# S4D convolution by FFT and gated MLP, f32: exchanges by quarters placed one by one, a decay table of 27 values, and a new order of the first phase

## The chip, the cores and the metric

One core of a Trainium2 chip runs the kernel; everything is f32. The metric is the device time of one execution in microseconds, as the median of several runs. Beside it there is one profiled execution, from which every duration below comes.

## What is computed

`x` is 2048 x 512. A layernorm, a long convolution per channel whose kernel is a sum of 128 decaying oscillations, and then a gMLP block with a spatial product over the sequence:

```python
P = jnp.exp((A * dt[:, None])[:, :, None] * pos)       # A = -exp(log_A_real) + i A_imag
K = 2.0 * jnp.einsum("dn,dnl->dl", C, P).real          # the convolution kernel of each channel
y = jnp.fft.irfft(jnp.fft.rfft(u_t, L2) * jnp.fft.rfft(K, L2), L2)[:, :, :L]
h = x + y + u * D_skip                                  # u is layernorm(x)
z = gelu(layernorm(h) @ w_in); z1, z2 = z[..., :Fh], layernorm(z[..., Fh:])
return h + (z1 * (w_sp @ z2 + b_sp)) @ w_out
```

## The kernel before

The change lies in the first phase, `phase_a`, which does the convolution; the three phases behind it (products with `w_in`, the second half of it with its norm, and the spatial product with the output) are as they were, and their lines have numbers smaller by 7 in the changed file (the line of the loads of `xq` is L715 before and L708 after).

The channels go in four chunks `c`. Per chunk:

- `params` turns the raw parameters into rates, phases and weights; three words per oscillation go to DRAM and come back through `stack` into `sw`. `table` makes `mt`, 64 by 34 values per partition: GpSimd multiplies the decay rates by a list of 34 distances (`c_lt`, three instructions), ScalarE takes the Exp, GpSimd multiplies four of the columns by the weights.
- Eight `unit`s (numbered `su` = 0 to 31 over all chunks) make the convolution kernel: a matmul for the phases (`ps<-c_k,sw`), Sin on ScalarE, three products of `mt` columns on GpSimd (`wa<-mt`), products on VectorE (`f`, `wa`) and GpSimd (`wb`), and two groups of 16 small matmuls (`ps<-f` and `ps<-wa,wb`), whose sum goes to a `ks` tile.
- `norm_x` normalises the input; 64 of its rows go to ScalarE or to GpSimd, one by one. `piece_a` and `piece_b` are the two matmul steps of the forward transform of the input, `piece_c` (`ps<-wb,ks`) and `piece_d` (`ps<-big,a`) those of the convolution kernel. Behind each `piece_d` its result is multiplied into the input's spectrum in `trio`, by VectorE; in chunk 3 three of the eight pieces are copied by ScalarE and multiplied by GpSimd, two instructions each. `piece_e` (`ps<-c_inv,trio`) is the inverse transform.
- `exchange(c)` swaps the two halves of the partitions of the input's spectrum, from one third of `trio` into another: 2 MB by DMA from SBUF to SBUF. Up is partitions 64 to 127 into 0 to 63, down the reverse; each in four quarters by `d`. All multiplies of `piece_d(c)` need it. Its target is still read by `piece_e(c-1)`: quarter q by the pieces `e(c-1, 2q)` and `e(c-1, 2q+1)`.

The order is not that of the code. `phase_a` records its operations in a `Plan`; a `group` counts as one operation. `RANKS` gives each its place, `FORMS` the engine where a copy or a normalised row may go to two, `BANKS` the PSUM bank. Up to `cut`, the last operation that touches the tiles which the next phase's loads will overwrite, all five queues are issued in that order. Then `phase_b1` issues its loads on SyncE: xq0, g0, xq1, g1 (a megabyte each), four quarters of w1r (448 KB each), xq2. Only then the rest of the plan is issued, with SyncE's instructions no longer held to the plan's order, and among it pieces of the split of w1r.

In `exchange`, the down half (a group) gets a dependency on the last DMA of the up half; SyncE waits there until that has landed. This is the key `after` in `issue`.

All recorded operations show the one line L252 (L251 after) in the profile.

Of the kernel before, what the change touches and what calls it, by code (L numbers as in the profile page):

```python
# [12 lines left out]
AF = mybir.ActivationFunctionType  # L13
# [24 lines left out]
    "06030B0I2U0Z0s10111I1N1j2619344U5V21000D0201050407080A090F0G0K0L0N0U0a0c0i0k0E0n1B0t0u0M0v14161A1G1d0O0Q0P0Y0b0dA10p0w0q"  # L38
    "1217181F1P1c1k1z282H2Q1e2X2R2V2v350r1H1J1L1s1-0H0C0W0l0J0V1E1m0R1t3G2Y3g3f0S1Y0X1Z234S4Y0T1i1f2g2s0o0e0j0g0m0x0f0h0z130y"
    "0-1Q0+1D151n1S1O1X1M1W1K1C1q1R1o1l1b1U1a1V1x1y24292A2z2B2C2G2J2N2T2Z2c2e2k2m2q2u2+2y3Z3W3l323B3A37333L3a314a4C4k393I3K4T"  # L40
    "67494B4N3e4A4G5x3J383y3b4j3V43483H2l2-1h272a3M3O1w2D2L1r1v2K3S2w1u2d3P2S2O2o2E2h2i2M3R2p3Q2t3N2W3E3T3U3X3Y3k3j3m3n3o3q3w"
    "3x3-42454F4I4P4V4b4W4f4n4z524c6f4s5c5P4q736u4t4-4v4m4o5E6O536e5U6v5v6o606n6U575D5a5+5C4g59867q7z9S9Q1T1p2P303i3u3z3+1g22"
    "20252F2IE82j2x2r3C3D3c3d3p404D4E4M4d6V4e5t4R5T708D3F365e7A7b7e46474X5g6N6Y6g7O7P5F5G5H5M5X5zJv6A6j6T6x7M7N7S7Y7d7j7t7u9-"
    "BB8hAKBJBKBLBeCmE27B7l8UBDBgBzBUBfBt5k5l6K6L5Q5S5N5O5R5Y5u5w5Z5d62636r728F8G7L7R8O8P7p807n7o8R8S6S6Z8V9u2f1+2n4J4O4l3h3t"
    "3v4H4w4Z4x4y6-8a8b2b3s4K4h4i4p3r41444Q564r5K5L5f7v814u584+515455505A5I5B5s5W5y5-7i9W9d5J5b5m5h5i5j5n5o5q5p6B616E6J797w85"
    "7F784L7f7Q7+7-5r6D6G68696P6C6F6X6W6a6b6c6i7C8M8N646d6M65666H6Q6R6q6k6t6s6y758I9V9X7g6h6w87888K6p767H7E8W7I8d8f8x94956I6z"
    "6+6l6m717V7W7m7k7r7x828C8l92938T8E7c9b7h9v9w8n8s7T7U7y8B74777X7Z7J7K7a7s7D7G8y9A8t919D9E9f9m9Y9ZANAOAQAU9k9oA8A9AqB2B1B6"
    "9sA6ASATABAC9rA29n9zCaCwBIBYBrBsCoC+BvCBCYCjCWCeBuCKCpDI8L8e8z8i8j8k8q968u9L8v8-98909M9i9jBFBP8J8483898A8X8Z8H8g8Q8c8Y8o"
    "8m8r8wAEBcC09N9a9P9K9T9U9e9c9p9g9q9l9y9tAGAJB3BVBW9F9H998p8+979B9C9G9O9J9I9x9R9+A0BMBaBbBZBjAj9hBqC8CCAmAMAVAZAaAbAwAeA+"
    "AvArAxB9B4BGBHDrDvD+AHADA5A3A4A7AWAAAIAgAPAFAlAXAnAsCEDADBBoBmBkBdBhBiB+BwBpC3BnBlC1B-C4CGCfDZDaB5ApAoA-B0B8BNBQBECABCBA"  # L50
    "C2BOCHCJCVDWDXC9C7BXC6BTCFChAfAkAhALARAYAyAzB7AcAiAdBRBSCZAtAuBxD7D8D9ByC5EnDsDxEQEbEDERDVDfDEDLDUDYF0F1DkDqExEyEkElEHEt"
    "D-EBECEPEWEeEmEwE7EGFEFFGDGJFRG0FrG2GaGdG5GCGYGZFXFlGiGtCDCRCUCQCkClCzCqCxCrCvD5DCD6DGDHDJEvE+COCTCICLCMCNCgCSCPCXCcCbCd"
    "CnCsC-DMFpFuCyDRDcDODPDQDhDSDdDjDeDmDuDpDzEEFZFaFoCiCuCtD0D1D2DFD3DDD4DNDKDbDTDiDlEuFIFJEgETEFFdEYFeFiEAEIELDwE9ENEdEKEO"
    "EMEXEZEcEfEoEpHCHDHGE5E0DtDgDnDoDyEJE6ESE3E1EaE4EhEiEjGkGlEVEzF2EqErEsFCF4F5FPE-F3FQFDFYFcG8GeGfEUFGFKFHFLFSFvFWFVFjFbFT"
    "GFFwGLGXH7HAHBGwFmFBGKGbHiHjF6F8F7F9FAFMFNFUFOFfFsFgFqFxFtFzF+GPGmGrGcGjGsG-HIHLI9IAHgHxGuH1HHHYHkHvH8H9HrHtHQHhHsHuHyHz"
    "HmHnHPHlH+IBHoHqIHIXIjIsIkIxIGIZIEIFITIeIbIoICIDIlImFyFkFhF-G3G4GEG6G7GAG9GGGHGIGUGWJGJOJWFnGOGSG1GMGNGgGpGRH2GQGTGqGhH3"
    "H4HXJ2J3GBGVGyGnGvGxHEH0G+HOH5GzHNHJHbHcIYJ9JVHMHTHRGoH6HFHZHKHVHaHUHSHWHdHeHfHwH-I0HpIUIKI7IPIQIpIaISIrIVIRIuItIvIyJHJd"
    "JeI4I6IMI1I2IIIcI3IJI5ILINIWIdIfIzI-JIJXI+J4JFJ5J7J8JRJPJJJQJLJMJNJSJTJUJYJZJaIOIiInI8IgIhIwIqJAJ0J1J6JBJCJDJEJKJbJcJuJw"
    "JfJgJhJrJkJpJjJmJqJnJiJoJlJxJ+JzJyJ-JsJtKCKEK2K9K6KFK3KAK0K1K7K8K4K5KBKD"
)  # L60
FORMS = (
    "000000001010100011000011100100000101100000011000001000000111001100110000100000000000100111100001010101101111101000000001"
    "00000110110110010100000100100100001110010100000010000001000110001101001101100000000101101110001001100000111001101111"
)
BANKS = (
    "414220313014444030432220022044434342124120412142014001422000123112321121011031223434430243400423134324420430131103321432"
    "034214411300222000123324434132420203334344321432242224410132113203001432002102101211314313432104023143234243141003422442"
    "030104322301034014314303413333144024"
# [3 lines left out]
def constants():  # L72
# [40 lines left out]
    for i in range(8):  # L113
# [9 lines left out]
        24 - 8 * np.arange(4), 1 + np.arange(7), 7 - np.arange(8), 64 * (1 + np.arange(7)),  # L123
        32 + 8 * np.arange(4), 512 * np.arange(4),
    ]).astype(f8)
    c["c_lt"] = np.broadcast_to(-lt, (P, 34))
# [62 lines left out]
class Plan:  # L189
# [59 lines left out]
    def issue(self, o):  # L249
        r = None  # L250
        for e, method, args, kw in o["calls"]:  # L251
            r = getattr(getattr(self.nc, e), method)(*map(self.real, args), **{k: self.real(x) for k, x in kw.items()})  # L252
            if "after" in o:
                info = mybir.DependencyInfo(mybir.DependencyClass.Sync, mybir.DependencyReason.DATA)
                self.tc.add_manual_dep(r.ins, o["after"]["ins"].name, info, reason="half by half")
        o["ins"] = r.ins
        return r
# [1047 lines left out]
```

## Time and profile before

| | us |
|---|---|
| runs | 813.02, 815.15, 815.5; median 815.15 |
| the profiled execution | 815.59 |
| its span | 813.8 |
| first phase, by the end of e(3) | about 274 of the span |
| PE busy over the span | 766.2 |
| granted TensorE clock, mean | 0.993 |

PE is TensorE's matmuls, PEld its weight loads, which overlap; DVE is VectorE, ACT ScalarE, POOL GpSimd, SP SyncE, and SPq SyncE's queue, whose rows are DMA issues. A row of a timeline has start, length, instruction, and in brackets the idle time of the engine just before it with what ended it. `out<-in` names the tiles; one name stands for several buffers.

### The profile page before, as it was taken

How to read it: one execution, taken by the hardware profiler on the slowest of the kernel's cores; microseconds unless marked ns; L12 is line 12 of the kernel's file. 1: busy time of each engine (PE TensorE's matmuls, PEld its weight loads, DVE VectorE, ACT ScalarE, POOL GpSimd, SP SyncE). 2: the span in 40 equal slices, each digit the busy share in tenths (PEclk: the TensorE clock that was granted, in tenths of full speed). 3: DMA queues.
4: the chain of work that ended last, by engine and by line, in shares of the span. 5: the costliest groups of instructions: out<-in, count | busy, mean ns of one | idle time of the engine just before them, and what ended most of it. 6: DMA issues, size and time to landing. Idle time of an engine off the chain costs nothing.

```text
span 813.8 us, 20008 instructions
## 1 busy us (share of the span) xinstructions
PE 766.2 (94%) x8081; PEld 651.5 (80%) x8081; DVE 593.7 (73%) x1155; ACT 452.0 (56%) x809; POOL 308.2 (38%) x356
## 2 busy tenths in 40 slices
PE   2489999999988989999999999999999999999998
PEld 1257888889978977888999888888888888888887
DVE  8998987976663587652586799978848993887534
ACT  8999989788652394562232455564345442454111
POOL 8999999978455100000421002233221002231200
PEclk9999999999997999999999999999999999999999
DMA  7604514415049256542450247999898548799542
GB/s 260 210 13 155 120 44 109 111 51 108 11 93 398 81 129 173 141 170 91 122 152 11 79 128 177 204 213 238 169 225 212 154 132 191 167 254 259 126 116 78
DMA packets 65004, 119.48 MB, mean 147 GB/s; under 512 B 6800, under 2 KB 21264, under 8 KB 63632
## 3 DMA queue, kind: packets, MB, share of 16 engines
q1 hardware_dynamic: 53248, 96.71, 39.5%
q0 software_dynamic: 11664, 21.50, 16.2%
q8 instruction: 63, 1.03, 0.5%
q14 instruction: 29, 0.24, 0.1%
HBM read 90.40 MB, written 19.40 MB: 135 GB/s over the span
## 4 chain that ended last, share of the span: by engine, by line
PE 83%; ACT 7%; DVE 7%; issue 2%; POOL 1%; DMA 0%; DVEq 0%; ACTq 0%; POOLq 0%
PE m L1192 34%; PE ps L252 20%; PE pz L987 9%; PE pz L882 8%; PE po L1115 7%; PE pl L1115 2%; DVE trio L252 2%; ACT ps L252 2%; ACT big L252 2%; PE y L756 1%; ACT wb L252 1%; DVE f L252 1%; DVE ps L252 1%; POOL wa L252 1%; DVE big L252 1%
## 5 line engine op out<-in xcount | busy, mean ns | idle before, releaser
L1192 PE MATMUL m<-wts,zc_wa 128*128 128x512 f32 x700 | 221.3, 395 | 0.0
L1192 PEld LDWEIGHTS m<-wts,zc_wa 128*128 128x128 f32 x700 | 131.8, 188 | 31.1 <-DVE c L1207 0.4
L1063 POOL DMA_DIRECT2D raws<-in_w_sp_dram x64 | 58.1, 991 | 211.7 <-DMA raws<-in_w_sp_dram 205.3
L1192 PE MATMUL m<-wts,zc_wb 128*128 128x512 f32 x350 | 138.2, 395 | 0.0
L252 POOL TENSOR_TENSOR wa<-mt 128x512 f32<-128x512 f32 x96 | 106.6, 1127 | 12.3 <-DVE big L252 4.2
L690 ACT CAST wts<-raws 128x512 fp32r<-128x512 f32 x112 | 68.9, 619 | 50.6 <-PE m L1192 24.5
L691 DVE TENSOR_TENSOR wts<-raws,wts 128x512 fp32r<-128x512 f32 x112 | 76.9, 689 | 17.1 <-ACT wts L690 17.0
L1192 PEld LDWEIGHTS m<-wts,zc_wb 128*128 128x128 f32 x350 | 65.9, 188 | 15.4
L987 PE MATMUL pz<-w,ht 128*128 128x448 f32 x384 | 77.0, 362 | 0.0
L987 PEld LDWEIGHTS pz<-w,ht 128*128 128x128 f32 x384 | 72.1, 188 | 4.8
L882 PE MATMUL pz<-ht,w1h 128*128 128x512 f32 (+1 forms) x248 | 73.8, 377 | 1.0 <-ACT ht L839 0.7
L993 POOL TENSOR_SCALAR sm<-sm 128x1 f32<-128x1 f32 x16 | 5.4, 336 | 159.9 <-DVE sm L992 159.9
L690 ACT CAST zc_wa<-raws 128x384 fp32r<-128x384 f32 (+1 forms) x70 | 37.1, 533 | 46.7 <-DVE raws L1097 28.0
L252 PE MATMUL ps<-c_inv,trio 128*128 128x128 f32 x512 | 60.8, 278 | 1.9 <-DVE trio L252 1.4
L1115 PE MATMUL po<-w,gz 128*128 128x512 f32 x252 | 61.8, 393 | 0.0
L252 PEld LDWEIGHTS ps<-c_inv,trio 128*128 128x128 f32 x512 | 58.5, 192 | 3.3 <-POOL trio L252 1.6
L252 PE MATMUL ps<-big,a 128*128 128x128 f32 x448 | 57.9, 287 | 1.2 <-ACT big L252 0.7
L252 DVE TENSOR_TENSOR f<-ps,wa 128x512 f32<-128x512 f32 (+1 forms) x64 | 46.9, 752 | 14.5 <-ACT ps L252 12.7
L252 PEld LDWEIGHTS ps<-big,a 128*128 128x128 f32 x448 | 54.2, 199 | 3.6 <-DVE trio L252 0.9
L1115 PEld LDWEIGHTS po<-w,gz 128*128 128x128 f32 x252 | 47.3, 188 | 10.9 <-DVE zo L1155 0.4
L882 PEld LDWEIGHTS pz<-ht,w1h 128*128 128x128 f32 x248 | 45.2, 189 | 10.8 <-ACT ht L839 1.4
L1097 DVE TENSOR_TENSOR raws<-z 128x384 f32<-128x384 f32 (+1 forms) x80 | 45.9, 582 | 0.3
(158 smaller groups left out, 1437.4 us busy)
## 6 DMA issues: line engine op xcount, KB each, us to landing
raws<-in_w_sp_dram SPq DMA_DIRECT2D x112, 256.0 KB, 4.0
raws<-in_w_sp_dram POOLq DMA_DIRECT2D x80, 256.0 KB, 5.8
trio<-trio SPq DMA_DIRECT2D x32, 256.0 KB, 3.8
scr_z<-zo SPq DMA_DIRECT2D x28, 256.0 KB, 2.1
big<-in_u_a_dram SPq DMA_DIRECT2D x8, 512.0 KB, 5.9
xq<-in_u_b_dram SPq DMA_DIRECT2D x4, 1024.0 KB, 8.9
g<-in_c_g_dram SPq DMA_DIRECT2D x4, 1024.0 KB, 8.9
scr_h<-xq SPq DMA_DIRECT2D x16, 256.0 KB, 4.1
```

Of the source, the lines that this page charges most:

```text
L252: r = getattr(getattr(self.nc, e), method)(*map(self.real, args), **{k: self.real(x) for k, x in kw.items()})
L690: nc.scalar.copy(hi, src)
L691: (engine or nc.vector).tensor_tensor(lo, src, hi.bitcast(F32), op=ALU.subtract)
L756: nc.tensor.matmul(ys[n, g][o:o + 64, i, :], gs[n][w, l, r], qv[w, r, 16 * n + l], start=(r == 0), stop=(r == 1), tile_position=(64 * h, o))
L882: nc.tensor.matmul(pt[:, w], a[:, q, f], ht[n][k][:, q, w], start=((q, i) == terms[0]), stop=((q, i) == terms[-1]))
L987: nc.tensor.matmul(pt[:, :FQ], a[:, q], w2[:, b, q, f], start=(q == 0 and i == 0), stop=(q == 3 and i == 2))
L993: nc.gpsimd.tensor_scalar_add(sm[:, 14:15], sm[:, 13:14], 1e-5)
L1063: nc.gpsimd.dma_start(r, ws[1], accum_op=ALU.add)
L1097: nc.vector.tensor_tensor(zs[:, :w], x, y, op=op)
L1115: nc.tensor.matmul(pt, gz[fb][x][:, P * a:P * a + P], wo[:, y, fb, w], start=(first and fb == fbs[0] and i == 0), stop=(last and fb == fbs ...
L1192: nc.tensor.matmul(pt, x[:, f], y, start=(k == 0 and i == 0), stop=(k == KT - 1 and i == 2))
```

## The change

1. `exchange` records eight operations where it recorded two groups of four. Up and down come in turn, quarter by quarter; the dependency of the down half on the up half is gone, and each of the eight has its own rank.
2. `c_lt` has 27 columns instead of 34: the two runs 1 to 7 and 7 to 0 shared values, and the second is now read backwards. The three GpSimd products of a table and the Exp shrink to 27/34.
3. In `params` the two sines stay in PSUM, and the three products with them go from GpSimd to VectorE.
4. `RANKS`, `FORMS` and `BANKS` are new throughout. In `FORMS`, 27 of the 64 normalised rows go to GpSimd instead of 23. ScalarE loads 19 activation tables in the first phase instead of 16.

```diff
 RANKS = (
-    "06030B0I2U0Z0s10111I1N1j2619344U5V21000D0201050407080A090F0G0K0L0N0U0a0c0i0k0E0n1B0t0u0M0v14161A1G1d0O0Q0P0Y0b0dA10p0w0q"
+    "0G020k0p2i0K0a0-111S1a1-220b4b3x3Q0J05010B000A1004070806090C0D0E0F0R0S0T0c0e0I0g0n0i0j0H0m14151F1G1I0L0N0M0O0P0Q2O0X0Z0Y"
...
     lt = np.concatenate([
-        24 - 8 * np.arange(4), 1 + np.arange(7), 7 - np.arange(8), 64 * (1 + np.arange(7)),
-        32 + 8 * np.arange(4), 512 * np.arange(4),
+        24 - 8 * np.arange(4), 1 + np.arange(7), 64 * np.arange(8), 32 + 8 * np.arange(4), 512 * np.arange(4),
     ]).astype(f8)
...
-            if "after" in o:
-                info = mybir.DependencyInfo(mybir.DependencyClass.Sync, mybir.DependencyReason.DATA)
-                self.tc.add_manual_dep(r.ins, o["after"]["ins"].name, info, reason="half by half")
...
-        si = ai
+        si, cp = bank("si", [P, N]), bank("co", [P, N])
...
-        nc.scalar.activation(co, a, AF.Sin, bias=half_pi)
+        nc.scalar.activation(cp, a, AF.Sin, bias=half_pi)
...
-        nc.gpsimd.tensor_tensor(co, co, mx, op=ALU.mult)
-        nc.gpsimd.tensor_tensor(si, si, mn, op=ALU.mult)
-        nc.gpsimd.tensor_tensor(co, co, si, op=ALU.add)
+        nc.vector.tensor_mul(co, cp, mx)
+        nc.vector.tensor_mul(si, si, mn)
+        nc.vector.tensor_add(co, si, co)
...
-        for i, (a0, b0) in ((2, (18, 30)), (0, (3, 26)), (1, (11, 0))):
-            ta = mt[:, d0:d0 + 16, a0:a0 + 8].unsqueeze(2).to_broadcast([P, 16, 4, 8])
+        for i, (a, b0) in ((2, (slice(11, 19), 23)), (0, (slice(3, 11), 19)), (1, (slice(10, 2, -1), 0))):
+            ta = mt[:, d0:d0 + 16, a].unsqueeze(2).to_broadcast([P, 16, 4, 8])
...
     def exchange(c):
         a, b, _ = spectra(c)
-        for o, i in ((0, 64), (64, 0)):
-            with nc.group():
-                for d in range(0, 32, 8):
-                    nc.sync.dma_start(b[o:o + 64, d:d + 8], a[i:i + 64, d:d + 8])
-        nc.ops[-1]["after"] = nc.ops[-2]
+        for d in range(0, 32, 8):
+            for o, i in ((0, 64), (64, 0)):
+                nc.sync.dma_start(b[o:o + 64, d:d + 8], a[i:i + 64, d:d + 8])
```

The built order shows what the new ranks move. SyncE's queue at the end of the first phase, before; the first row is the whole of exchange(2), the third the whole of exchange(3), and behind it come the loads of the next phase:

```order
L252 DMA trio<-trio 64x1024 x8
L252 DMA sw_90<-scr_stk 48x1024
L252 DMA trio<-trio 64x1024 x8
L715 DMA xq_3724<-in_u_b_dram 128x2048
L718 DMA g_3728<-in_c_g_dram 128x2048
L715 DMA xq_3725<-in_u_b_dram 128x2048
L718 DMA g_3729<-in_c_g_dram 128x2048
L725 DMA w1r<-in_w_dram 128x896 x4
L715 DMA xq_3726<-in_u_b_dram 128x2048
L718 DMA g_3846<-in_c_g_dram 128x2048
```

The same place after; the row of 14 holds the eight of exchange(2) and six of exchange(3):

```order
L251 DMA sw_90<-scr_stk 48x1024 x2
L251 DMA trio<-trio 64x1024 x14
L708 DMA xq_3684<-in_u_b_dram 128x2048
L711 DMA g_3688<-in_c_g_dram 128x2048
L708 DMA xq_3685<-in_u_b_dram 128x2048
L711 DMA g_3689<-in_c_g_dram 128x2048
L718 DMA w1r<-in_w_dram 128x896 x4
L708 DMA xq_3686<-in_u_b_dram 128x2048
L251 DMA trio<-trio 64x1024 x2
L711 DMA g_3846<-in_c_g_dram 128x2048
L711 DMA g_3848<-in_c_g_dram 128x2048
```

The last two quarters of exchange(3), quarter 1 up and down (of `e(2,2)` and `e(2,3)`), stand behind the nine loads: their ranks lie behind the cut. The last two of the six ahead of the loads are those of quarter 0, which wait for `e(2,1)`. Of the two behind, the first also waits for the DMA slot of g0 and the second for that of xq1.

TensorE from `e(2,1)` on, before; `ps<-c_inv,trio` is `piece_e`, `f` and `wa,wb` are a unit's two products, `wb,ks` is `piece_c`, `c_k` the phases:

```order
L252 MATMUL ps_100<-c_inv,trio 128x128 x8
L252 MATMUL ps_99<-c_inv,trio 128x128 x8
L252 MATMUL ps_100<-f_94 32x64 x16
L252 MATMUL ps_100<-wa,wb 32x64 x16
L252 MATMUL ps_99<-wb,ks_81 64x2x32 x16
L252 MATMUL ps_97<-c_k,sw_90 128x512 x2
L252 MATMUL ps_99<-wb,ks_82 64x2x32 x16
L252 MATMUL ps_100<-f_94 32x64 x16
L252 MATMUL ps_100<-wa,wb 32x64 x16
L252 MATMUL ps_98<-wb,ks_85 64x2x32 x16
L252 MATMUL ps_101<-f_93 32x64 x16
L252 MATMUL ps_97<-wb,ks_80 64x2x32 x16
```

Four more rows follow before `piece_d` of chunk 3: one product `wa,wb` and three `piece_c`. After, from `e(2,1)` on, with the first `piece_d` as the last row:

```order
L251 MATMUL ps_99<-c_inv,trio 128x128 x8
L251 MATMUL ps_100<-f_93 32x64 x16
L251 MATMUL ps_98<-f_94 32x64 x16
L251 MATMUL ps_100<-wa,wb 32x64 x16
L251 MATMUL ps_101<-c_inv,trio 128x128 x8
L251 MATMUL ps_100<-c_inv,trio 128x128 x8
L251 MATMUL ps_97<-wb,ks_82 64x2x32 x16
L251 MATMUL ps_98<-wa,wb 32x64 x16
L251 MATMUL ps_99<-wb,ks_80 64x2x32 x16
L251 MATMUL ps_97<-wb,ks_85 64x2x32 x16
L251 MATMUL ps_98<-wb,ks_81 64x2x32 x16
L251 MATMUL ps_99<-big,a_78 128x2x2x32 x4
```

More of the last two units now stands ahead of `e(2,1)`, and `e(2,3)` stands behind it beside `e(2,2)`.

ScalarE in the head, before; `mt` rows are the Exp of a table, `big<-big,trio` normalised rows:

```order
L252 ACT_TABLE_LOAD
L252 ACTIVATE mt_91<-mt_91 128x2176
L252 CAST trio<-trio 128x128
...
L252 ACTIVATE mt_92<-mt_92 128x2176
L252 ACT_TABLE_LOAD
L252 ACTIVATE ps_101<-ps_101 128x128
L252 ACT_TABLE_LOAD
```

After, where the second table stands behind most of the normalised rows with two loads of its own:

```order
L251 ACTIVATE mt_91<-mt_91 128x1728
...
L251 ACTIVATE ps_98<-ps_98 128x1024
L251 ACTIVATE big<-big,trio 128x2x48 x2
L251 ACT_TABLE_LOAD
L251 ACTIVATE mt_92<-mt_92 128x1728
L251 ACT_TABLE_LOAD
L251 ACTIVATE ps_97<-ps_97 128x1024
```

Up to the second Exp and the load behind it that makes six table loads before and seven after.

## What it will do to the time: the prediction

> **What bounds the kernel now.** I read the page's engine table and its chain first, then the windows by stage, then the timelines of SyncE's queue and of TensorE where the first phase ends, with the landings of the DMAs there.
>
> ```profile
> span 813.8 us, 20008 instructions
> PE 766.2 (94%) x8081; PEld 651.5 (80%) x8081; DVE 593.7 (73%) x1155; ACT 452.0 (56%) x809; POOL 308.2 (38%) x356
> ...
> 0.00:64.00 64.00, 32.89 (x715) 23.08 (x718) 57.86 (x179) 59.49 (x132) 60.10 (x76) 1.00 0.50 158
> 64.00:235.00 171.00, 168.14 (x4005) 152.09 (x4000) 134.35 (x179) 142.76 (x203) 143.18 (x150) 1.00 0.34 85
> 235.00:260.00 25.00, 19.13 (x397) 17.04 (x389) 13.38 (x16) 9.14 (x15) 13.02 (x15) 0.80 0.92 307
> ```
>
> A window row has the stretch and its length, then the busy time of PE, PE's weight load, DVE, ACT and POOL, then the granted clock, the DMA share and GB/s. TensorE bounds the whole, and the change adds and drops no matmul. So it can pay or cost only where PE idles, and it touches the first phase alone. PE idles there in two places: the head (32.9 of 64 us busy, with ACT, DVE and POOL all at 58 to 60) and the tail (19.1 of 25, clock 0.80). Between them it works 168.1 of 171 us.
>
> The tail is the last exchange, the eight DMAs that feed chunk 3's multiplies and then its inverse transforms. SyncE's queue first (start, length, instruction), then PE:
>
> ```profile
> 231.66 10.68 SPq L252 DMA_DIRECT2D trio<-trio  x8
> 242.45 1.13 SPq L715 DMA_DIRECT2D xq<-in_u_b_dram  x1
> 243.70 1.19 SPq L718 DMA_DIRECT2D g<-in_c_g_dram  x1
> 244.98 0.40 SPq L715 DMA_DIRECT2D xq<-in_u_b_dram  x1
> 245.43 1.22 SPq L718 DMA_DIRECT2D g<-in_c_g_dram  x1
> 246.75 1.85 SPq L725 DMA_DIRECT2D w1r<-in_w_dram  x4
> 249.97 0.33 SPq L715 DMA_DIRECT2D xq<-in_u_b_dram  x1
> ...
> 229.54 3.84 PE L252 MATMUL ps<-c_inv,trio 128*128 128x128 f32 x32
> 233.31 0.66 PE L252 MATMUL ps<-f 128*32 128x64 f32 x32
> 234.41 0.70 PE L252 MATMUL ps<-wb,ks 64*64 64x64 f32 x32
> 235.23 0.73 PE L252 MATMUL ps<-c_k,sw 128*128 128x512 f32 x2
> 240.84 0.65 PE L252 MATMUL ps<-f 128*32 128x64 f32 x32 [1.75 <-DVE f L252]
> 247.78 8.75 PE L252 MATMUL ps<-big,a 128*128 128x128 f32 x56 [0.70 <-ACT big L252]
> ...
> 259.59 14.66 PE L252 MATMUL ps<-c_inv,trio 128*128 128x128 f32 x128 [1.41 <-DVE trio L252]
> ```
>
> The first PE row holds e(2,1) and e(2,2), 1.92 us each. The end of e(2,1) releases the exchange at 231.66; call that moment X. The first e(3) starts at 259.59, so 27.9 us after X. All of e(3) needs all of the exchange. The next phase's loads stand behind it in the same queue.
>
> **The tail in the changed order.** SyncE's rows in the section on the change show that six of the eight DMAs stand ahead of the loads and two, quarter 1 up and down, behind xq0, g0, xq1, g1, the four w1r and xq2. Of those six, the last two need e(2,1), the moment X; the loads follow. Its DMAs are of these sizes (KB each, then the median us from issue to landing):
>
> ```profile
> xq<-in_u_b_dram SPq DMA_DIRECT2D x3, 1024.0 KB, 10.3
> ...
> w1r<-in_w_dram SPq DMA_DIRECT2D x4, 448.0 KB, 13.2
> trio<-trio SPq DMA_DIRECT2D x3, 256.0 KB, 3.7
> ```
>
> So the last two DMAs now come after 6.75 MB of loads (five of a megabyte and 1.75 of w1r). Their price, from these rows:
>
> ```profile
> DMA to landing us min/median/max: 2.9/5.5/14.8
> ...
> SPq L715 <- DMA xq<-in_u_b_dram: 1.3, 1, 1.3
> ...
> 242.00:244.00 2.00, 1.20 (x41) 0.87 (x32) 0.65 (x3) 1.07 (x2) 0.03 (x1) 0.56 1.02 211
> 244.00:246.00 2.00, 1.76 (x65) 1.77 (x68) 0.99 (x2) 0.00 (x0) 0.18 (x1) 0.50 1.02 223
> ...
> 250.00:252.00 2.00, 2.00 (x12) 2.00 (x11) 0.40 (x1) 0.52 (x1) 1.27 (x1) 0.50 1.02 426
> 252.00:254.00 2.00, 2.00 (x17) 2.00 (x17) 0.93 (x2) 0.69 (x2) 0.34 (x1) 0.88 1.01 418
> ```
>
> Step by step after X:
> - Two issues at 0.46 us (four w1r take 1.85): xq0 is issued at X+1.0.
> - xq0's landing (first row: the times of the xq loads). The ends are 2.9 us, the least, and 7.5: in before xq2's issue waited for xq0 to land (second row) and came at 249.97, 7.5 us after xq0's issue, with most of a megabyte of the down half ahead of it. With half as much ahead I take the median, 5.5: X+6.5.
> - From xq0's landing to xq2's. In before xq2, issued at 249.97, took the longest, 14.8, and landed at 264.8; that is 14.8 after xq0. The loads between fill the engines (share 1.02, 426 GB/s), so the same here: X+21.3.
> - The pair, 0.52 MB. At the rate that the window with the down half under way shows, 211 to 223 GB/s, 2.4 us; at the loads' 426, 1.2. I take 2.4: X+23.7.
>
> The multiplies follow:
>
> ```profile
> L252 POOL TENSOR_TENSOR trio<-trio 128x512 f32<-128x512 f32 x6 | 7.5, 1276 | 8.2 <-ACT trio L252 8.2
> ...
> L252 DVE TENSOR_TENSOR trio<-ps,trio 128x1024 f32<-128x1024 f32 x5 | 6.0, 1222 | 7.2 <-PE ps L252 7.1
> ```
>
> - POOL's six at 1.276 make 7.7 us; DVE's five at 1.222 make 6.1, with three pieces of PE waiting for their banks in between. No row shows how soon they start after a landing; between 0 and 3 us I take 1. e(3) starts at X+32.4 instead of X+27.9: **+4.5**, with ends near +1 and +8.
> - X itself moves. PE's rows in the section on the change show, between e(2,1) and the first piece of d(3), before: one e (1.92), six products (0.66 each), seven pieces of c (0.70 each), one phase (0.73), 11.5 us; after: two e, four products, four c, 9.3. The 2.2 us of difference now stand ahead of X: **+2.2**.
> - The clock. In before it was 0.50 from about 242 to 252, after a PE gap of 1.75 us, and came back some 4.7 us into the run that starts at 247.78. Here PE would stand idle for most of 15 us before e(3), whose 14.66 us ran at full clock. At half clock for 4.7 us it would lose 2.3; at best nothing. I take the middle, **+1.2**.
>
> Work that is gained there: before's gaps of 1.75 and 0.70 us and its half clock vanish, but they lie inside the 27.9 us that are replaced, so they are no term.
>
> **The head.** These groups are of 0 to 64 us (busy time, then mean ns of one):
>
> ```profile
> L252 POOL TENSOR_TENSOR mt<-wb 128x816 f32<-128x816 f32 (+1 forms) x7 | 10.1, 1463 | 1.2 <-ACT wb L252 1.1
> L252 ACT ACTIVATE mt<-mt 128x2176 f32<-128x2176 f32 x2 | 4.0, 2016 | 0.0
> L252 ACT ACT_TABLE_LOAD x6 | 7.7, 1283 | 0.8 <-PEq L1299 0.7
> L252 ACT ACTIVATE big<-big,trio 128x96 f32<-128x96 f32 x41 | 18.5, 547 | 0.1
> L252 POOL TENSOR_SCALAR big<-big,trio 128x96 f32<-128x96 f32 x23 | 16.7, 783 | 0.0
> L252 POOL TENSOR_TENSOR trio<-trio 128x128 f32<-128x128 f32 x12 | 5.3, 448 | 0.4 <-ACT trio L252 0.2
> L252 DVE SCALAR_TENSOR_TENSOR trio<-trio,ps 128x128 f32<-128x128 f32 (+1 forms) x6 | 1.6, 270 | 0.0
> ```
>
> The table shrinks to 27/34: POOL −2.1 us, ACT −0.8. Three products of the first parameters leave POOL (−1.3) for DVE (+0.8 at the nearest row, 270 ns). Four normalised rows move from ACT (−2.2) to POOL (+3.1). ACT gets one table load more, since its second Exp now stands apart from the first (+1.3). So ACT gains 1.7, POOL 0.3, and DVE loses 0.8 before the choices of engine for the copies, which give DVE six more in the phase, at 0.69 each:
>
> ```profile
> L252 DVE COPY big<-ps 128x512 f32<-128x512 f32 x12 | 8.1, 687 | 13.6 <-PE ps L252 13.6
> ```
>
> The ends: if ACT alone decided, and its saving came through whole with the earlier first units, up to 3 us gained; if the nearly full DVE decides, which takes those six as well, 4 lost. I take **+1**. Later parts of this saving lie beside a PE that is 98% busy: nothing.
>
> **The alternating halves.** Dropping the wait of the down half saves SyncE 13.2 us in all:
>
> ```profile
> SPq L252 <- DMA trio<-trio: 13.2, 4, 4.1
> ```
>
> Three of the four lie under the saturated PE, and the fourth is inside the 27.9 us. Costed at nothing; if the cover were gone, 9.1 us for the three (13.2 less 4.1). Alternation itself moves no byte faster here: one half alone already shows a DMA share of 1.02. The Trainium skill, "SBUF — State Buffer", section "Can I just issue two DMAs to hit both halves?", says the same against this change: a DMA at partition 0 and one at partition 64 together measured only 6% over one. By it an exchange would be 6% shorter at most, which changes no term.
>
> **The sum.** 4.5 + 2.2 + 1.2 + 1.0 = 8.9 us. The profiled execution took 815.59 (span 813.8 and what lies around it), which gives 824.5; it was 0.44 above the median of the runs, 815.15, so 824.1 for the median.
>
> **The rivals.**
> - *The pair passes the loads* (0.12). Its issue waits for a free DMA slot, the landings of g0 and of xq1, two megabytes at 2.5 us after xq0's, so X+11.5. If it landed 2.4 to 3.7 us later beside the loads, X+14.5, then 1 and 7.7: X+23.2, which is 4.7 less than before; with 2.2 for X and 1 for the head that is −1.5, so 813.6 for the median, not slower; and with a head that gains 3 where I let it cost 1, 809.6. It decides if the pair lands before about X+16. Against it: the loads landed one after another in before, xq2 14.8 us after its issue though a megabyte needs 2.5 at 426 GB/s. The Trainium skill, "DMA: Bandwidth & Descriptors", section "Queues, rings and completion order", has each engine take descriptors in ring order but lets a later one finish its write first. By that, a small pair could slip a little, not past six megabytes; the trace shows no such overtaking.
> - *The head pays* (0.09). The first unit's parameters and table are ready earlier and PE fills its 31 idle us in the head better: 4 us better than my +1 and no half clock in e(3), 819. Against it: DVE and POOL are full there as well.
> - *The waits between the halves were on the path* (0.03): 9.1 less than the sum, 815.0. Against it stands the window of 64 to 235 us.
> - *The head costs* (0.10): DVE's extra work sets the pace until PE is full, +4 instead of +1, and POOL's multiplies start 2 us late: 829.
>
> **How the numbers follow.** The forecast as it stands has 0.66. Its terms' ends give 817 to 831; the first rival lies below. The range 815.5 to 831 leaves out most of the first rival and a little above, under 2 in 10. A measurement of this kernel can tell about 0.3%, 2.4 us, from no change. Faster comes from half of the first rival (with a head that does not cost) and from the second with the lowest ends of the tail: 0.08; the same from the other half of the first, and from the third: 0.08; slower 0.84.
>
> **What would show it.** Right: in the trace after, two trio DMAs on SyncE's queue behind xq2, issued some 12 to 15 us after X and landing some 24 after it; DVE's and POOL's multiplies with an idle stretch before them that a trio DMA ends; PE idle for about 15 us before the first e(3), which starts near X+32; a window of low granted clock there; the second phase then of unchanged length. Wrong: if the multiplies begin within 16 us of X, if the first e(3) starts before X+28, or if PE reaches its saturated stretch over 3 us earlier than 64 us.

## The result, and the profile after

The changed kernel took 841.1 us (median of 4 runs, 839.8 to 843.65), against 814.72 for the kernel before in runs beside it: a ratio of 1.0317 [1.0291, 1.0344]. The loss of 26 us is three times the forecast of 8.9, and the time lies above the range's end of 831. The profiled execution of after took 840.79 us. Its page:

```profile
span 839.0 us, 19995 instructions
...
PE 768.2 (92%) x8081; PEld 653.2 (78%) x8081; DVE 600.5 (72%) x1170; ACT 448.6 (53%) x802; POOL 298.7 (36%) x351
```

TensorE's work is nearly what it was (768.2 us against 766.2), so some 23 of the 25 us of span are idle time. The windows of after show where (stretch, length, busy PE, PEld, DVE, ACT, POOL, clock, DMA share, GB/s):

```profile
0.00:20.00 20.00, 2.67 (x8) 1.58 (x8) 15.96 (x86) 14.13 (x33) 10.75 (x16) 1.00 0.78 266
20.00:40.00 20.00, 7.18 (x21) 5.37 (x21) 15.22 (x63) 13.02 (x35) 16.77 (x21) 1.00 0.61 181
40.00:60.00 20.00, 14.05 (x385) 10.37 (x389) 18.60 (x25) 19.74 (x41) 19.41 (x24) 0.91 0.23 58
...
64.00:232.00 168.00, 160.75 (x3930) 141.98 (x3931) 140.45 (x188) 140.36 (x199) 137.95 (x153) 1.00 0.32 83
...
260.00:280.00 20.00, 5.85 (x36) 5.66 (x36) 3.49 (x3) 1.23 (x3) 4.71 (x4) 0.68 0.65 234
```

And the same stretches of before:

```profile
0.00:20.00 20.00, 4.11 (x13) 2.76 (x13) 16.18 (x87) 15.95 (x34) 17.81 (x24) 1.00 0.77 261
20.00:40.00 20.00, 8.87 (x81) 5.84 (x82) 18.92 (x66) 19.54 (x50) 18.37 (x24) 1.00 0.69 217
40.00:60.00 20.00, 16.37 (x527) 11.45 (x530) 18.79 (x23) 20.00 (x42) 19.93 (x25) 1.00 0.02 5
...
64.00:232.00 168.00, 165.14 (x3899) 149.34 (x3895) 131.48 (x175) 140.55 (x199) 140.84 (x149) 1.00 0.33 84
```

All three parts of the first phase lose: the head, the middle, which the forecast held saturated, and the tail. To put a size on each, the next table lays TensorE's work of the first phase end to end (its groups of matmuls at their full-clock lengths, 237 us) and gives the moment at which each point is reached, in us of the span. It is worked out from the timelines; the last four columns belong to runs told below.

| work done | before | after | alternating | pair late | old head | all three |
|---|---|---|---|---|---|---|
| 0 | 27.7 | 31.2 | 28.1 | 27.8 | 27.4 | 27.3 |
| 24 | 62.8 | 72.3 | 63.2 | 62.9 | 66.1 | 66.1 |
| 110 | 146.9 | 157.3 | 147.3 | 146.7 | 150.9 | 151.2 |
| 150 | 184.3 | 198.4 | 186.2 | 184.1 | 192.1 | 191.3 |
| 200 | 231.4 | 246.3 | 233.2 | 231.1 | 239.8 | 239.4 |
| 234 | 272.3 | 297.8 | 277.2 | 287.2 | 292.2 | 274.7 |

After is 9.5 us late at 24, 14.9 at 200, 25.5 at 234. **The head costs 9.5, the middle 5.4, the tail 10.6.** Behind it the second phase is as long as it was: it starts at 300.46 instead of 274.97.

The tail, after, first SyncE's queue, then PE, then DVE and POOL:

```profile
249.43 0.90 SPq L708 DMA_DIRECT2D xq<-in_u_b_dram  x1
...
257.83 0.33 SPq L708 DMA_DIRECT2D xq<-in_u_b_dram  x1
260.37 2.92 SPq L251 DMA_DIRECT2D trio<-trio  x2
...
240.95 7.30 PE L251 MATMUL ps<-c_inv,trio 128*128 128x128 f32 x64
...
276.54 5.08 PE L251 MATMUL ps<-big,a 128*128 128x128 f32 x24 [14.11 <-DVE trio L251]
283.10 10.96 PE L251 MATMUL ps<-c_inv,trio 128*128 128x128 f32 x96 [1.48 <-DVE trio L251]
295.94 3.84 PE L251 MATMUL ps<-c_inv,trio 128*128 128x128 f32 x32 [1.89 <-ACT big L251]
...
275.26 3.49 DVE L251 TENSOR_TENSOR trio<-ps,trio 128x1024 f32<-128x1024 f32 x3 [19.17 <-DMA trio<-trio]
...
275.29 7.43 POOL L251 TENSOR_TENSOR trio<-trio 128x512 f32<-128x512 f32 x6 [19.80 <-DMA trio<-trio]
```

X, the end of e(2,1), is 248.2. The pair's two issues come at X+12.2 and X+14.6, right behind the landings of g0 (260.30) and xq1 (262.80). VectorE and GpSimd idle until 275.3, X+27.1, and e(3) starts at X+34.9 (before: X+27.9). That is the forecast's mechanism, and the marks that it named are there, with the landing and e(3) some 3 us later than it gave.

The head, after, SyncE, GpSimd and PE:

```profile
21.93 0.42 SPq L251 DMA_DIRECT2D a<-in_c_a_dram  x1
...
10.54 3.50 POOL L251 TENSOR_TENSOR mt<-wb 128x648 f32<-128x648 f32 x3 [6.02 <-ACT wb L251]
...
21.29 0.74 POOL L251 DMA_DIRECT2D c_k<-in_c_k_dram  x1
...
31.17 2.90 PE L251 MATMUL ps<-c_k,sw 128*128 128x512 f32 x6 [9.65 <-DMA c_k<-in_c_k_dram]
```

Before, the table's products began at 5.75 and the 2 MB of `a` were issued 11.6 us behind c_k:

```profile
29.69 0.42 SPq L252 DMA_DIRECT2D a<-in_c_a_dram  x1
...
5.75 4.24 POOL L252 TENSOR_TENSOR mt<-wb 128x816 f32<-128x816 f32 x3 [1.12 <-ACT wb L252]
...
18.06 0.74 POOL L252 DMA_DIRECT2D c_k<-in_c_k_dram  x1
```

c_k's load, as the landings of 0 to 45 us have it (KB, us from issue to landing), after:

```profile
c_k<-in_c_k_dram POOLq DMA_DIRECT2D x1, 512.0 KB, 9.8
```

and before:

```profile
c_k<-in_c_k_dram POOLq DMA_DIRECT2D x1, 512.0 KB, 4.0
```

The middle: TensorE's waits from 64 to 232 us (in all, times, longest), after:

```profile
PE ps L251 <- issue: 3.3, 4, 1.7
PE ps L251 <- DMA wa<-scr_xhat: 1.1, 2, 0.9
```

and before, where that wait was short:

```profile
PE ps L252 <- issue: 0.3, 1, 0.3
```

"Issue" means that no semaphore explains the wait. This row had no counterpart in the forecast.

### The profile page after: what moved, and what is told of

It is laid out like the page before. It is cut to its first block, busy times and chain, and to the rows that moved or that the text cites. A ratio compares the mean times of both kernels' runs of the same rounds, so it can differ in the third digit from the quotient of the medians.

```text
span 839.0 us, 19995 instructions
## 1 busy us (share of the span) xinstructions
PE 768.2 (92%) x8081; PEld 653.2 (78%) x8081; DVE 600.5 (72%) x1170; ACT 448.6 (53%) x802; POOL 298.7 (36%) x351
## 3 DMA queue, kind: packets, MB, share of 16 engines
q8 instruction: 63, 1.03, 0.5%
## 4 chain that ended last, share of the span: by engine, by line
PE 76%; DMA 7%; ACT 6%; DVE 5%; issue 2%; POOL 2%; SPq 1%; DVEq 0%; ACTq 0%; POOLq 0%
PE m L1185 33%; PE ps L251 16%; PE pz L980 9%; PE pz L875 7%; PE po L1108 7%; PE pl L1108 2%; DMA trio<-trio 2%; DVE trio L251 2%; DVE f L251 1%; DMA xq<-in_u_b_dram 1%; DMA c_k<-in_c_k_dram 1%; PE y L749 1%; SPq L251 1%; ACT ps L251 1%; ACT big L251 1%
## 5 line engine op out<-in xcount | busy, mean ns | idle before, releaser
L251 POOL TENSOR_TENSOR wa<-mt 128x512 f32<-128x512 f32 x96 | 104.3, 1107 | 17.0 <-ACT mt L251 8.1
L251 PE MATMUL ps<-big,a 128*128 128x128 f32 x448 | 59.1, 288 | 15.8 <-DVE trio L251 14.1
L875 PEld LDWEIGHTS pz<-ht,w1h 128*128 128x128 f32 x248 | 45.2, 189 | 10.8 <-ACT ht L832 1.4
L251 DVE TENSOR_TENSOR trio<-ps,trio 128x1024 f32<-128x1024 f32 (+1 forms) x35 | 36.1, 1057 | 23.7 <-DMA trio<-trio 20.6
```

The costliest lines, as they stand in the source:

```text
L875: nc.tensor.matmul(pt[:, w], a[:, q, f], ht[n][k][:, q, w], start=((q, i) == terms[0]), stop=((q, i) == terms[-1]))
```

## The experiments

Each ratio is to runs of the kernel before that were made beside the run (medians 814.66 to 815.64).

**The tail.** First the pair moved ahead of the loads, everything else as in after:

```diff
+    pair = ex3[2:4]
...
+    order = rest_of[:at] + pair + rest_of[at:]     # behind the other six of exchange(3)
```

> The changed kernel with one thing moved: the last two DMAs of exchange(3) are issued ahead of the nine loads of the next phase. Theory (the queue): the multiplies of chunk 3 waited until 275.2 us for these two, which stood behind 6.75 MB. Ahead of the loads they can be issued when e(2,2) ends, at about 253.5, and land near 258; then 1 + 7.7 us of multiplies, so the first e(3) at about 267 instead of 283.1: 16 us less than the changed kernel, about 825 us (822 to 828). Rival (something else holds the multiplies or what follows, such as the loads themselves, which now come 5 us later): under 6 us less, above 835 us.

828.64 us (826.62 to 829.93), ratio 1.0171 [1.0141, 1.02]: 12.5 us less than after, just short of what was expected. Timeline, POOL and PE:

```profile
263.20 7.43 POOL L251 TENSOR_TENSOR trio<-trio 128x512 f32<-128x512 f32 x6 [3.85 <-DMA trio<-trio]
...
270.68 10.98 PE L251 MATMUL ps<-c_inv,trio 128*128 128x128 f32 x96 [2.33 <-POOL trio L251]
```

X was 252.0 in this run, so e(3) starts at X+18.6: the late place costs 16 us there. X to e(3) is then also 9.3 us shorter than in before. The profiled run's span, 828.2, is 10.8 shorter than that of after, since X came 3.8 later (head and middle were longer) and e(3) to y (the first product of the second phase) took 19.0 us instead of 17.4.

The counterpart puts the late pair into the kernel before:

```diff
+    pair = [o["calls"].pop(1) for o in ex3]        # quarter 1, up and down
...
     load_x(2)
+    pair()
```

> The kernel before with one thing moved: quarter 1, up and down, of exchange(3) is issued behind xq2, as in the changed kernel. Theory (the queue): the loads start a little earlier than before, at about 241, the pair lands two megabyte-loads behind g1 and w1r, at about 266, and e(3) starts near 275 instead of 259.6: 14 to 17 us more, about 830 us (827 to 833). Rival (a pair issued when g0 and xq1 have landed passes the loads): lands near 256, 4 to 6 us more, about 820 us. Second rival (the wait is covered by other work): 815 us.

829.03 us (828.13 to 830.84), 1.0187 [1.0161, 1.0212]. In this run seven of the 11 multiplies stood ahead of the pair in the program and took quarter 1 unexchanged, without waiting for it. So it was made again with all 11 behind the pair, which a dummy operation that marks the `cut` moved forward brings:

```diff
+    order.remove(tail[0])
+    order.insert(1256, tail[0])
```

> As e3_before_pair_late, the kernel before with quarter 1 of exchange(3) behind xq2, but now all eleven multiplies of chunk 3 wait for it; in e3 seven of them were issued ahead of the pair and took quarter 1 as it was before the exchange, so that they did not wait, and that run was a lower end. Theory (the queue): the pair lands near 268, as in e3, 7.7 us of multiplies follow, e(3) starts near 276 instead of 259.6: about 833 us (831 to 836). Rival (the pair passes the loads): about 820 us.

830.28 us (829.84 to 830.85), 1.018 [1.0162, 1.0199]: +14.9, just under the theory's range and far from its rival. Timeline, SyncE's queue, PE, DVE:

```profile
250.64 2.96 SPq L252 DMA_DIRECT2D trio<-trio  x2
...
272.95 16.23 PE L252 MATMUL ps<-c_inv,trio 128*128 128x128 f32 x128 [1.41 <-DVE trio L252]
...
265.93 4.62 DVE L252 TENSOR_TENSOR trio<-ps,trio 128x1024 f32<-128x1024 f32 x4 [20.17 <-DMA trio<-trio]
```

The column "pair late" of the table shows that nothing moved ahead of the tail. Of the 14.9 us, 13.4 lie ahead of e(3); the rest is e(3) itself, 16.23 us instead of 14.66, at a granted clock of 0.90. In SyncE's queue the pair passes no load: in both kernels it lands some 15 us behind its issue, behind xq2 (after: 275.0 against 273.9; here 265.7 against 264.5). For that queue the rival is out.

Is it SyncE's queue that holds the pair? The next run issues it from ScalarE:

```diff
+    for o in pair:
+        o["calls"] = [("scalar", *call[1:]) for call in o["calls"]]
```

> The changed kernel with the last pair of exchange(3) issued from ScalarE's queue, at the time that e(2,2) allows it, about 254 us, while the loads of the next phase are under way from SyncE's. Theory (the pair waited in the order of SyncE's queue, and two queues share the engines): it lands near 260, e(3) starts near 269, about 827 us (825 to 830). Rival (the DMA engines take what was issued first, whatever the queue): it lands behind w1r, near 271, about 838 us.

839.92 us (837.57 to 843.92), 1.0311 [1.0276, 1.0345]: about 1 us. Timeline, ScalarE, then PE:

```profile
259.90 3.09 ACTq L251 DMA_DIRECT2D trio<-trio  x2
263.04 1.07 ACT L251 COPY big<-ps 128x512 f32<-128x512 f32 x2 [7.55 <-DMA xq<-in_u_b_dram]
...
279.47 12.61 PE L251 MATMUL ps<-c_inv,trio 128*128 128x128 f32 x96 [3.05 <-POOL trio L251]
```

The pair's inputs (e(2,3)) were ready at 254.2, but its two DMAs were issued at 259.90 and 262.52, 0.02 us behind the landings of g0 (259.88) and xq1 (262.50): the wait for a free slot goes with the DMA and not with the queue. From there the pair did get ahead of loads that were issued before it: it landed at 267.8 and 271.7, xq2 at 275.3. Counted from X (248.9 here), e(3) came at X+30.6 instead of X+34.9. But ScalarE's copies stood behind the pair for 7.5 us, and the second phase began only 2.0 us earlier (298.49). Between the medians 1.2 us are left, which the intervals do not tell from nothing. What the pair needs most is its place in the order of issue, ahead of the loads.

**The head.** One load moved, c_k ahead of everything on GpSimd:

```diff
+    moved = [o for o in order if o["calls"][0][0] == "gpsimd" and o["calls"][0][1] == "dma_start"]
...
+    order.remove(moved[0])
+    order.insert(0, moved[0])
```

> The changed kernel with only the load of c_k moved to the front of GpSimd's queue (it was issued at 21.29 us, together with the 2 MB of a on SyncE's queue, and landed at 31.1; the first phases wait for it, while ScalarE and VectorE idle for 4.4 us). Theory (a DMA in the head): the first phases come at about 25 us and the idle 4.4 us are won through to the end, about 837 us (835 to 838.5). Rival (the head is bound by the work of ScalarE and VectorE, and by where the new order puts it): that work fills the gap later, 0 to 1 us, 840 to 841 us.

838.5 us (838.11 to 839.55), 1.0302 [1.0278, 1.0326]: −2.6 between the medians, −1.2 by the ratios, whose intervals overlap. The phases start at once where the data is there, but little else does (PE's timeline):

```profile
26.70 3.30 PE L251 MATMUL ps<-c_k,sw 128*128 128x512 f32 x6 [4.16 <-DVE trio L251]
```

After 24 us of work it is still 6.3 us late. Together with the edit of the pair:

> The changed kernel with both: the last pair of exchange(3) ahead of the loads and the load of c_k at the front of GpSimd's queue. Theory (two separate stretches, whose prices add): 828.6 less 2.6, about 826 us (824.5 to 827). Rival (what the head gains is lost again on the way to the tail): 828.6 us.

825.72 us (821.55 to 828.86), 1.0121 [1.0087, 1.0155]: 2.9 less than the pair alone. That fits two prices that add up, but the four runs spread over 7 us. Three suspects for the rest of the head. First, on top of e2, the loads of `ident` and `c_lt` ahead of the input's, and the first copy of the rates ahead of ScalarE's second table load:

```diff
+    lead = [swap, *evacs]
...
+    order[at:at] = lead
...
+    order[at:at] = front
```

> The changed kernel with the load of c_k at the front of GpSimd's queue, the loads of ident and c_lt ahead of the input's, and the first copy of the rates ahead of ScalarE's second table load; the late pair stays. In the changed kernel GpSimd idles for 6 us before its first table product at 10.5 us (5.75 before), and the head is 6 us late even with c_k early. Theory (that late first table is what the rest of the head's lateness comes from): 3 to 5 us less than e2_ck_early's 838.5, about 834.5 us. Rival (the order of ScalarE and VectorE from 30 us on, with the second Exp and its two table loads there, makes it): 0 to 1.5 us less, about 838 us.

840.4 us (837.34 to 841.52), 1.0297 [1.0269, 1.0324]: the table's products now begin at 7.29 instead of e2's 11.64, and that brings nothing beside e2's 838.5. The theory of the late first table falls. Next the second Exp, with its two table loads, moved into ScalarE's idle stretch of 4.4 us in after:

```diff
+    order.remove(exps[0])
...
+    order.insert(max(before, fed + 1), exps[0])
```

> The changed kernel with one instruction moved: the second table's Exp, with its two table loads, goes ahead of the first unit's sines, into the 4.4 us in which ScalarE idles until c_k has landed, instead of to 45.5 to 49.7 us. Theory (ScalarE's order in the head is what is left of its lateness): about the 4.2 us of the three, less what the sines wait, 3 to 4 us less than the changed kernel, about 837.5 us. Rival (VectorE and GpSimd hold the pace there): 840 to 841 us.

841.76 us (838.72 to 843.65), 1.0326 [1.0299, 1.0353]: nothing, though the Exp now runs at 29.41 instead of 46.77; its place is not it either. Then the price of the added loads on the kernel before, by an Exp of one element:

```diff
+    order.insert(at[4], dict(calls=[("scalar", "activation", (dummy, half_pi, AF.Exp), {})], names=set(), rank=-1))
```

> The kernel before with an Exp of one element put into ScalarE's order in the head, in the middle of the units' sines, which costs two activation table loads more, 2.6 us, and 0.2 for itself. Theory (ScalarE sets the pace there, so that its time comes through to the end): 815.4 plus 2.8, about 818.2 us (817.3 to 819.5). Rival (another engine sets it, or the time is won back before TensorE is full): 815 to 816.5 us.

818.14 us (814.81 to 820.24, 12 runs), 1.0023 [1.0002, 1.0044]: one pair of table loads more in ScalarE's head costs the kernel before about 2 us. The changed kernel has one load more there, not two.

The table of 27 values alone, on the kernel before:

```diff
-    c["c_lt"] = np.broadcast_to(-lt, (P, 34))
+    c["c_lt"] = np.broadcast_to(-lt, (P, 27))
...
```

> The kernel before with the table of 27 values alone (shorter products on GpSimd and a shorter Exp in each table; the order, the engines and all else as before). Theory (the tables lie beside other work, except for the first two in the head): 0 to 2 us less, about 814 us. Rival (the head runs at ScalarE's and GpSimd's pace, so that the saving comes through): 3 us less or more, under 812 us.

814.81 us (12 runs), 0.9994 [0.9971, 1.0017]: nothing.

Then the whole head as it was, the first 430 operations in before's order, engines and banks, and the products of `params` back on GpSimd, all later operations as changed. Beside the tables of numbers:

```diff
-        nc.vector.tensor_mul(co, cp, mx)
+        nc.gpsimd.tensor_tensor(co, co, mx, op=ALU.mult)
...
```

> The changed kernel (27 values, its order, its exchanges, the late pair) with the head of the kernel before: the first 430 operations of the order, about the first 60 us, stand in the order, on the engines and in the banks of before, the three products of the parameters are on GpSimd again, and everything else follows in the changed order. Theory (the order of the head as a whole, not one load or one Exp, costs the 9.6 us by which TensorE is behind after 24 us of its work): they are won, about 831.5 us (829 to 834). Rival (the head's lateness is work done early for later; without it the middle pays): above 836 us.

837.64 us (835.44 to 838.38), 1.028 [1.0243, 1.0318]: 3.5 us less than after between the medians, the rival's side. (The profiled executions lie 5.4 apart; this one was the fastest of its kernel.) It keeps step with before up to 20 us of work and loses 3.3 at once (row 24) where the changed order takes over. PE's timeline there:

```profile
59.40 0.65 PE L251 MATMUL ps<-wa,f 128*32 128x64 f32 x32 [0.47 <-DVE wa L251]
61.45 0.33 PE L251 MATMUL ps<-ident,trio 128*128 128x128 f32 x1 [1.40 <-ACT trio L251]
62.34 1.16 PE L251 MATMUL ps<-trio,a 128*128 128x128 f32 x8 [0.56 <-ACT wb L251]
```

Before has that transpose at 69.77, without a wait, and other work in its place.

**The middle.** The halves in turn without the wait, on the kernel before:

```diff
-        for o, i in ((0, 64), (64, 0)):
+        for half in ((0, 8), (16, 24)):
             with nc.group():
-                for d in range(0, 32, 8):
+                for d in half:
+                    for o, i in ((0, 64), (64, 0)):
...
-        nc.ops[-1]["after"] = nc.ops[-2]
```

> The kernel before with the first part of the change alone: up and down in turn by quarters, no wait between them, at the places of the two groups. Theory (the waits lie beside a saturated TensorE, and the transfers fill the engines either way): 814.5 to 816 us. Rival 1 (a wait of 4.1 us was on the path at the tail): 811.5 us. Rival 2 (eight DMAs at once hold up something that TensorE needs, such as the 3.3 us of waits without a releaser that the changed kernel shows between 64 and 232 us against 0.3 before): 2 us more or above, over 817.5 us.

820.06 us (818.01 to 823.23), 1.0059 [1.0038, 1.008]: 4.6 us lost. What the forecast costed at nothing, and whose wait it even counted as a possible gain, does harm. The waits of 64 to 275 us and the two places (PE's timeline):

```profile
PE ps L252 <- issue: 2.4, 2, 1.4
```

```profile
150.90 1.83 PE L252 MATMUL ps<-big,a 128*128 128x128 f32 x15 [1.37 <-issue]
...
240.62 0.42 PE L252 MATMUL ps<-wa,wb 128*32 128x64 f32 x12 [0.99 <-issue]
```

The table's column "alternating" steps by 1.5 between 110 and 150, where the first of them lies, and by 3.1 in the tail, where the second lies. The second wait is only 0.99 of these 3.1; beside it e(3) ran at a lower clock (0.89 at 259 to 275 us, before 1.00). The reverse gives exchanges 0 to 2 of e5 a wait again, the last four DMAs for the landing of the fourth:

```diff
+        if c < 3:
+            eights.append(nc.ops[-8:])
...
+        x[4]["after"] = x[3]
```

> As e5_pair_ck (the changed kernel with the last pair ahead of the loads and c_k early), and in exchanges 0 to 2 the last four of the eight DMAs wait until the fourth has landed. Theory (an exchange without a pause holds up something that TensorE needs to issue: waits without a releaser of 4.5 us in e5, 3.3 in the changed kernel, 0.5 in the one before): most of these go, 2 to 4 us less than e5's 825.7, about 822.7 us. Rival (they come from the order, or from other transfers): 825.7 us, or up to 2 us more where the pause itself delays the multiplies.

822.54 us (819.2 to 823.08), 1.0083 [1.006, 1.0107]: 3.2 us less than e5, as expected, though the two kernels' runs overlap. The issue waits up to 245 us of e5:

```profile
PE ps L251 <- issue: 4.5, 6, 1.7
```

The same of e7, where the one at exchange(1) went from 1.73 to 0.22:

```profile
PE ps L251 <- issue: 3.0, 5, 1.1
```

All three repairs at once (e12's head, the pair ahead, the pauses):

> As e12_head_of_before, with the last pair of exchange(3) ahead of the loads and a pause in exchanges 0 to 2 as in e7_waits. Theory (head, pauses and late pair are the three causes, and their prices add): e12's time less some 16 us (e7 less e2), 815.5 us (813 to 818.5), the time of the kernel before. Rival (something else in the changed order's middle and tail costs): above 820 us.

819.81 us (817.57 to 824.3, 9 runs), 1.007 [1.0045, 1.0094], 21.3 less than after, between the theory and its rival. 4.8 us stay, and no version beats the kernel before.

What does TensorE wait for in an "issue" wait? The DMA records of the trace also hold transfers of a kind called instruction (63 on queue 8 in after, 1.03 MB by the page), of 16,384 bytes each. In ten runs (before, after, e3b, e5, e6, e7, e12, e13 and the two below) they were set beside TensorE's 38 issue waits of 60 to 262 us. All 38 end 1.25 to 1.62 us behind the end of such a transfer, for example (us of the span):

```
run          wait   transfer           TensorE goes on
after        1.71   160.74 to 161.71   163.10
after        0.72    91.38 to  92.65    94.21
e6           1.37   148.25 to 149.30   150.90
e6           0.99   238.10 to 239.02   240.62
e3b          0.89   236.04 to 237.00   238.40
```

The place is closer still. Count TensorE's instructions in the trace from the first, and the transfers from 0: in all 38 TensorE stops after exactly 256 n + 449 instructions, where n is the number of the transfer that it goes on behind. And 63 transfers of 256 make 16,128, about its 8081 matmuls and 8081 weight loads. So TensorE had run out of instructions. Two last runs ask what holds the transfer up. The first has the wait taken out and the halves as they were:

```diff
-        nc.ops[-1]["after"] = nc.ops[-2]
```

> The kernel before with the wait of the down half on the up half taken out of all four exchanges and nothing else: the halves still come one after the other, in their places. Theory: what the wait gives is a stretch of a few us in which the DMA engines are nearly empty (share 0.14 at 144 to 146 us of before), and in it TensorE's next 16 KB of instructions come in; without it TensorE waits for its instructions, as it did where the halves alternated (issue waits 2.4 us between 64 and 275, kernel 4.6 us slower). So about 819.5, 817.5 to 821, with issue waits of 1 us or more that end 1.2 to 1.7 us after the end of a transfer of kind instruction. Rival: alternation itself, up and down in turn, did the harm; then this gives 815, 813.5 to 816.5, with issue waits of about 0.5 as before.

817.89 us (814.03 to 819.32, 12 runs), 1.0026 [1.0008, 1.0044]. Its issue waits from 64 to 275 us:

```profile
PE ps L252 <- issue: 3.0, 5, 1.0
```

So the missing wait alone brings them; whether alternation adds to it (2 us between the medians of e6 and this) the intervals leave open. The profiled execution, 815.16, shows no loss, for another reason. Just ahead of e(3) the kernel before's ran at half clock and this one at full clock (its 56 matmuls `ps<-big,a` took 8.75 us before and 6.9 here). First before, then this run:

```profile
242.00:252.00 10.00, 8.26 (x157) 7.74 (x149) 2.24 (x5) 2.83 (x5) 1.48 (x2) 0.51 1.01 337
242.00:252.00 10.00, 6.33 (x211) 5.46 (x211) 4.86 (x7) 2.73 (x5) 1.90 (x3) 1.00 0.98 317
```

Compared at like clocks the loss is there: with a mean clock of 0.997 or more the medians are 815.71 against 813.17 for before, with a lower one 818.31 against 815.65. In the next run the pause is kept, but in exchanges 0 to 2 it is filled with another transfer:

```diff
+        o["calls"].insert(0, ("sync", "dma_start", (o["fill"], ins["u_b"][:, 1024 * c:1024 * c + 1024]), {}))
```

> The kernel before with its wait kept, and one more transfer of 512 KB, DRAM to DRAM, that nobody reads, issued on SyncE between the halves of exchanges 0 to 2 ahead of the wait: the pause is filled with traffic of another purpose. Theory: it is the empty DMA engines that let TensorE's instructions in, so issue waits come back, 1 us or more in all between 64 and 232 where before has 0.3, and the time is 816.5 to 820. Rival: the pause helps in another way (when the landings release the multiplies, or SyncE's own order); then issue waits stay at 0.3 to 0.5 and the time within 814 to 816.5.

814.81 us (812.76 to 817.8, 12 runs), 1.0004 [0.9987, 1.0021], and the waits are almost those of before:

```profile
PE ps L252 <- issue: 0.7, 2, 0.4
```

In the windows of exchange(1), before's DMA share shows the pause (0.14):

```profile
144.00:146.00 2.00, 2.00 (x26) 1.88 (x29) 1.90 (x3) 1.97 (x3) 2.00 (x5) 1.00 0.14 46
```

In e14 it is gone (1.02):

```profile
144.00:146.00 2.00, 2.00 (x18) 1.86 (x16) 1.90 (x3) 1.97 (x4) 2.00 (x5) 1.00 1.02 264
```

And in e15 it is filled:

```profile
144.00:146.00 2.00, 2.00 (x42) 1.52 (x41) 1.90 (x4) 1.96 (x5) 2.00 (x3) 1.00 1.00 227
146.00:148.00 2.00, 2.00 (x57) 1.88 (x59) 1.72 (x3) 1.97 (x3) 2.00 (x4) 1.00 0.81 268
```

The theory that empty DMA engines let the instructions in falls for exchange(1): e15 keeps them 81 to 100% busy there, and the wait of 0.96 us that e14 has there is gone. So it seems to be enough that the exchange's own eight DMAs do not run in one piece. Of e14's other waits three, 1.7 us in all, lie at exchange(3), whose pause e15 left empty; for these the theory was not tried.

## Why the prediction was wrong in size, point by point

- *The tail, +7.9 forecast, 10.6 measured: right in its mechanism.* e1 and e3b show it from both sides, and the first rival (the pair passes the loads) is out for SyncE's queue; from ScalarE's (e10) the pair did pass the last of them. The terms: X moved by 1.6 beyond the delay it inherits (16.5 less 14.9; forecast 2.2). X to e(3) grew by 7.0 (forecast 4.5). The mis-sized term is xq0: it landed 8.4 us after its issue where 5.5 was taken. That 5.5 was the median of a row that holds four stores from xq beside its loads; in before xq0 itself took 7.5. From xq0's landing to the first multiply it took 17.4 us (forecast 18.2). The last term was named wrongly: e(3) to y took 17.4 us instead of 15.4, not by a half clock (1.00 at 283 to 296) but by ScalarE, whose casts of w1r (292.79 to 295.41) stand ahead of the copy that PE waits for (1.89 us idle). The half clock did come, 0.68 at 260 to 280, while PE had little to do; in e3b it reached e(3).
- *The head, "I take +1", with ends of −3 and +4: it failed.* Measured 9.5. The step summed up busy times of three engines, and no term of it asks when an input arrives. One late input cost some time: c_k, which lands 9.8 us after its issue when `a` is queued 0.6 us behind it (e2: 2.6 us between the medians, 1.2 by the ratios; e5: 2.9). Another, GpSimd's first table products at 10.54 instead of 5.75, is as late but cost nothing (e8). In the first 40 us the three engines are less busy than before (POOL 27.5 against 36.2, ACT 27.2 against 35.5), and the work is left for later. No single place accounts for the rest (e8, e11: nothing). The old order of the head wins 3.5 in all (e12), so for most of the 9.5 the cause within the head stays open.
- *"The alternating halves. Costed at nothing": it failed.* 4.6 us on the kernel before (e6). The prediction looked for what the wait costs SyncE and did not ask what else comes by DMA meanwhile. Its third rival held the wait for a possible loss; on this kernel it protects.
- *"Later parts of this saving lie beside a PE that is 98% busy: nothing": it failed, and with it "it can pay or cost only where PE idles".* The middle lost 5.4 us. A full PE can hardly gain, but it can lose. 3.0 of it are issue waits (3.3 against 0.3), 1.1 waits for `xhat` loads. The changed order also brings TensorE to instructions whose inputs are not ready (e12: 1.40 and 0.56 us).
- *The savings in the head.* The 27 values, counted there with 2.1 us of GpSimd and 0.8 of ScalarE, were worth nothing (e4). The products on VectorE were not tried alone.

What stays open: of the 26.4 us, e13 accounts for 21.3. The 4.8 that are left lie by its trace in the changed order of the middle (3.3 at 24 us of work, 8.0 at 200, of which 5.6 come back in the tail), and no run took that order apart. Why an exchange in one piece holds up an instruction transfer, while as much other traffic in its pause does not, was not settled either.

## What to carry to other kernels

Look for small DMAs that the critical path needs and that stand behind bulk loads, and give them their place ahead of these; another queue helps little where the issue also waits for a slot that the loads hold. Before a wait is taken out or a transfer made denser, ask what else comes by DMA beside it, instructions included: a saturated engine gains nothing by the change and can lose. A stretch that is bound by several engines at once is not priced by adding up busy times; follow for each of them what it waits for first, and price a load with what is queued beside it.

## What was not expected of the hardware

- TensorE's instructions come by DMA, in transfers of 16,384 bytes, 36 between 60 and 260 us here, and TensorE stood still up to 1.7 us when one was late. The Trainium skill, "Runtime: NRT & Kernel Launch", section "Instruction fetch mechanics", has the instruction memory refilled in blocks of 16 KiB, 256 instructions, and this mostly hidden. The block's size and count agree with the trace's records. Mostly hidden holds too, for all but 38 of some 360 transfers in the ten runs; these cost up to 4.5 us a run. The four waits of after's middle all lie inside groups of small matmuls. By the row below, 32 of these and their 32 weight loads take 0.65 us, so 256 instructions last 2.6 us there, while no two transfers of after's first phase behind 60 us start less than 3.2 us apart:

```profile
237.70 0.65 PE L251 MATMUL ps<-f 128*32 128x64 f32 x32
```

- The Trainium skill, "DMA: Bandwidth & Descriptors", section "Queues, rings and completion order", has each DMA engine go round its rings packet by packet. By that, traffic in other rings should hold an instruction transfer up little once it is under way. The traces agree: the transfers take 0.9 to 1.7 us in all ten runs. What differs is their start. Counted as above, transfer 21, the one at exchange(1), starts when TensorE is 203 instructions past 256 n in before and 205 in e15, but 381 in e14 and 382 in e6, where TensorE then waits for it. What delays the start no run shows.
- The same 512 KB load took 4.0 us from issue to landing in before (DMA share 0.54 at 18 to 22 us) and 9.8 in after, with 2 MB queued 0.6 us behind it (share 1.07 at 21 to 31).
- A DMA on ScalarE's queue waited for slots that landings on SyncE's queue free, 259.9 instead of 254.2, and held up ScalarE's own copies. Behind its issue it was faster than on SyncE's queue: its two parts took 7.9 and 9.2 us to land (e10), against 14.1 and 12.2 (after).
